# Reciprocal deviation of a layer norm: Ln and Exp on ScalarE in place of a power on GpSimd, with a new order of the work

## The chip, the cores and the metric

The kernel runs on one core of a Trainium2 chip. The core has five engines that work in parallel, each through its own queue in order: TensorE (matmuls, "PE" in the profile), VectorE ("DVE"), ScalarE ("ACT"), GpSimd ("POOL") and SyncE ("SP"), which issues the transfers. The metric is the time of one execution on the device in microseconds; lower is better.

## What is computed

Two transformer layers over 2048 rows of width 512. Each has a sliding-window attention (32 heads of 16, window 256) and a feed-forward part with relu; both read a layer norm of x and add to x.

```
def _layernorm(x, axis=-1, eps=1e-5):
    m = jnp.mean(x, axis=axis, keepdims=True)
    v = jnp.var(x, axis=axis, keepdims=True)
    return (x - m) / jnp.sqrt(v + eps)
...
    x = x + _A_ref(_layernorm(x, axis=-1), A_wqkv, A_wo)
    x = x + _B_ref(_layernorm(x, axis=-1), B_w1, B_w2)
    x = x + _A_ref(_layernorm(x, axis=-1), A_wqkv, A_wo)
    x = x + _B_ref(_layernorm(x, axis=-1), B_w1, B_w2)
```

In `_A_ref` the scores of q and k are scaled by 1/4, masked to the window, put through a softmax, multiplied with v and with `wo`. `_B_ref` is `relu(x @ w1) @ w2` with 1792 columns between.

## The kernel before

Rows go in chunks of 512, four chunks a layer, so there are eight steps k (k = 0 to 3 are the first layer). For each step the program plans: the norm of the chunk and the projections to q, k and v (`plan_qkv`, lines 542 to 609); the attention in units of one group of heads, 36 units with up to five score groups each (`plan_attention`, from 611); the output projection, the second norm and the feed-forward part (`plan_rest`, from 682). All of x stays in on-chip memory (`x_sb`), as do the weights.

A score group is four by two or three matmuls into the one score buffer `Sps`, followed by one exponential on ScalarE into `Pb` (line 633). The next scores need the buffer, so scores and exponentials alternate. The masks of the window work on `Pb` after the exponential, on VectorE or GpSimd (lines 440 to 458). The matmuls of attention with v (`acc`) need a whole unit's exponentials and masks. Between two score groups TensorE does other matmuls, if any is ready: projections (`ps_d<-xnT,wqk` and `wv`), output projection (`wo`) and feed-forward (`ps_d<-xn2T,w` and `w,hT`).

The norm of a block of 128 rows is a chain over several engines. `norm_stats` (line 332) makes mean and variance on VectorE (`bn_stats`, `bn_aggr` into `mvs`) and, for every second block, adds eps to two variances into `rstds`. `norm_pow` (356) raises these to the power -0.5 on GpSimd, two blocks at once, against a constant tile `mhalf`. `norm_apply` (360) writes the normalised block `xn`: on VectorE one operation with mean and reciprocal deviation; on GpSimd two small operations first, which make the negative mean times the reciprocal deviation (`nbs`), then one that multiplies and adds. A transposing DMA (SyncE's queue) or, for the first and the last chunk, TensorE's transposes bring `xn` into `xnT` or `xn2T`, which the matmuls read.

The order on each engine is not written out by hand. Every operation is an `Op` with a key, the engines that may do it with a time for each, and what it waits for. A small simulation (lines 777 to 898) runs through time with these durations (`EVAC`, the times beside the operations), a time for a signal from one engine to another (`LINK`), one for a freed buffer to be usable again (0.2 us) and times for TensorE to turn from one kind of matmul to another (`SWITCH`). Whenever an engine is free it takes, of the operations that are ready, the one with the smallest key plus ready time (`choose`, line 806), and that is how instructions are written into its queue. Some 100 numbers in `TUNE` shift the keys: `calm` those of the statistics of a chunk in the first layer, `apply` those of the applies, `mask`, `div`, `qkv`, `v`, `h`, `add` those of their operations; `lead` lets attention's matmuls start so long ahead of an exponential's end, `hold` keeps other matmuls back just ahead of it, and `slack` says how far another operation on ScalarE may reach into the time of the next exponential (`act_free`, line 824). If TensorE finds nothing for some time, a filler matmul ("warm") is put in. On the chip the queues run in that order, and semaphores decide the real times. All instructions go through a helper, so that nearly every row of the profile names its line, 152.

Of the kernel before, what the change touches and what calls it, by code (L numbers as in the profile page):

```python
# [14 lines left out]
ALU = mybir.AluOpType  # L15
P = 128
# [37 lines left out]
    ("qkv", 6): -0.16, ("qkv", 7): -14.32,
    ("v", 0): 13.35, ("v", 1): 3.92, ("v", 2): 26.56, ("v", 3): 18.45, ("v", 4): -13.88, ("v", 5): 7.52,
    ("v", 6): 18.09, ("v", 7): 3.4,
    ("h", 0): -6.3, ("h", 1): 14.4, ("h", 2): -21.08, ("h", 3): 6.8, ("h", 4): 11.71, ("h", 5): -2.12,
    ("h", 6): 9.91, ("h", 7): -16.5,
    ("mask", 0): -22.35, ("mask", 1): 12.42, ("mask", 2): 0.91, ("mask", 3): 7.99, ("mask", 4): 9.44,
    ("mask", 5): -27.11, ("mask", 6): -3.69, ("mask", 7): 8.01,  # L60
    ("div", 0): -20.69, ("div", 1): -29.64, ("div", 2): -11.92, ("div", 3): -2.95, ("div", 4): 7.05,
# [7 lines left out]
    ("pace", 6): -1.08, ("pace", 7): 4.91,
    ("from", 1): 13.51, ("from", 2): 36.31, ("from", 3): 0.92, ("from", 4): 5.3, ("from", 5): 11.42,  # L70
    ("from", 6): -38.65, ("from", 7): 33.44, ("from", (0, 0)): 2.38, ("from", (0, 2)): -18.94,
    ("span", 1): 67.18, ("span", 2): 34.97, ("span", 3): 28.32, ("span", 4): 54.36, ("span", 5): 52.47,
    ("span", 6): 24.91, ("span", 7): 70.78, ("span", (0, 0)): 35.26, ("span", (0, 2)): 58.29,
# [35 lines left out]
def kernel(  # L109
# [133 lines left out]
    LINK = {"PE": 0.2, "DVE": 0.2, "ACT": 0.2, "POOL": 0.2, "SP": 0.2}  # L243
# [50 lines left out]
    d_x = [landed(3.95), landed(4.5)]  # L294
    d_w = {1: landed(7.4), 0: landed(9.0), 2: landed(10.6)}
# [64 lines left out]
    def norm_apply(lid, j, src, deps, by_array, dst, then_key, dst_deps):  # L360
# [20 lines left out]
        return op(0, {"SP": (1.22, dma, 2.9)}, [a], None, [box])  # L381

    def transpose(key, src, dst, deps, uses, take=None):
# [671 lines left out]
```

## Time and profile before

| | |
|---|---|
| median of 3 runs | 465.89 us (464.25 to 467.16) |
| profiled execution, its own time | 466.79 us |
| its span, first to last instruction | 465.1 us |
| TensorE busy, matmuls | 439.3 us, 94% |
| VectorE busy | 362.6 us, 78% |
| ScalarE busy | 342.7 us, 74% |
| GpSimd busy | 324.4 us, 70% |
| mean granted clock of TensorE | 0.979 |

One execution is taken by the profiler. A busy share is a mean over the whole span; the stretches differ, so a table of stretches is read beside it. The granted clock is the share of TensorE's full speed in a stretch. In a row of instructions, out<-in are tiles by their names in the program, then partitions x elements and the type; the bracket at the end of a row tells for how long the engine idled before it and which instruction ended the wait. "issue" is time in which an engine waited for nothing that the profile shows.

### The profile page before, as it was taken

How to read it: one execution, taken by the hardware profiler on the slowest of the kernel's cores; microseconds unless marked ns; L12 is line 12 of the kernel's file. 1: busy time of each engine (PE TensorE's matmuls, PEld its weight loads, DVE VectorE, ACT ScalarE, POOL GpSimd, SP SyncE). 2: the span in 40 equal slices, each digit the busy share in tenths (PEclk: the TensorE clock that was granted, in tenths of full speed). 3: DMA queues.
4: the chain of work that ended last, by engine and by line, in shares of the span. 5: the costliest groups of instructions: out<-in, count | busy, mean ns of one | idle time of the engine just before them, and what ended most of it. 6: DMA issues, size and time to landing. Idle time of an engine off the chain costs nothing.

```text
span 465.1 us, 15122 instructions
## 1 busy us (share of the span) xinstructions
PE 439.3 (94%) x6418; PEld 216.4 (47%) x6418; DVE 362.6 (78%) x760; ACT 342.7 (74%) x278; POOL 324.4 (70%) x671
## 2 busy tenths in 40 slices
PE   7949988989699999999999999999999999999995
PEld 3625454644245454444544444454444445444443
DVE  6898888887878789988889888867987898669201
ACT  3877988678778887788877787888879887760530
POOL 3665788876878798889888778855886787741000
PEclk9997999899889999999999999999999999999999
DMA  8806101010302100211011102000041001100001
GB/s 259 274 13 184 25 1 26 13 37 2 47 14 59 24 3 14 35 24 25 1 39 35 24 3 47 4 2 1 24 82 35 4 13 48 35 1 24 23 15 39
DMA packets 39580, 18.36 MB, mean 39 GB/s; under 512 B 30928, under 2 KB 38992, under 8 KB 39504
## 3 DMA queue, kind: packets, MB, share of 16 engines
q1 hardware_dynamic: 39504, 17.31, 14.8%
q8 instruction: 52, 0.85, 0.8%
q14 instruction: 24, 0.20, 0.2%
HBM read 7.86 MB, written 2.10 MB: 21 GB/s over the span
## 4 chain that ended last, share of the span: by engine, by line
PE 81%; POOL 7%; ACT 4%; DMA 3%; issue 2%; DVE 1%; SPq 0%; POOLq 0%; ACTq 0%
PE ps_d L152 63%; PE Sps L152 10%; PE acc L152 8%; ACT Pb L152 4%; POOL Pb L152 4%; DMA Pb<-in_A_wqkv_dram 2%; POOL xn L152 1%; DMA xnT<-xn 1%; DMA xn2T<-xn 1%; POOL nbs L152 1%; POOL rstds L152 0%; SPq L152 0%; DVE st L152 0%; PE tp L152 0%; ACT wv L152 0%
## 5 line engine op out<-in xcount | busy, mean ns | idle before, releaser
L152 ACT ACTIVATE Pb<-Sps 128x2048 bf16<-128x2048 f32 (+2 forms) x156 | 282.7, 1812 | 68.4 <-PE Sps L152 48.4
L152 POOL TENSOR_SCALAR_AFFINE_SELECT Pb<-Pb 64x256 bf16<-64x256 bf16 x516 | 237.0, 459 | 72.8 <-ACT Pb L152 45.5
L152 PE MATMUL ps_d<-xn2T,w 128*128 128x512 bf16 (+1 forms) x504 | 109.7, 360 | 1.1 <-DMA xn2T<-xn 1.1
L152 PE MATMUL ps_d<-w,hT 128*128 128x512 bf16 (+1 forms) x462 | 106.8, 374 | 0.0
L152 PE MATMUL Sps<-Qt,KBD 32*128 32x320 bf16 (+3 forms) x1488 | 62.1, 254 | 13.5 <-ACT Pb L152 13.3
L152 PEld LDWEIGHTS <-w 128*128 128x128 bf16 x504 | 45.6, 99 | 48.9 <-issue 10.1
L152 PE MATMUL ps_d<-xnT,wqk 128*128 128x512 bf16 (+1 forms) x288 | 66.2, 361 | 2.3 <-DVE st L152 1.8
L152 PEld LDWEIGHTS <-hT 128*128 128x128 bf16 x462 | 41.6, 98 | 48.6 <-issue 6.6
L152 DVE TENSOR_TENSOR Pb<-Pb,tri 128x512 bf16<-128x512 bf16 (+1 forms) x132 | 56.2, 441 | 6.2 <-ACT Pb L152 5.5
L152 PEld LDWEIGHTS <-KBD 32*128 32x128 bf16 x1488 | 27.1, 93 | 69.9 <-issue 67.6
L152 DVE STREAM_TRANSPOSE TR<-acc 128x512 f32<-128x512 f32 (+1 forms) x72 | 44.6, 639 | 18.1 <-PE acc L152 17.7
L152 DVE TENSOR_SCALAR hT<-ps_d 128x512 bf16<-128x512 f32 (+1 forms) x73 | 43.9, 607 | 12.8 <-PE ps_d L152 12.0
L152 PE MATMUL acc<-Pb,V2f 64*32 64x320 bf16 (+4 forms) x2976 | 46.5, 256 | 0.6 <-POOL Pb L152 0.6
L152 DVE BATCH_NORM_STATS2 st<-x_sb 128x6 f32<-128x512 f32 (+1 forms) x64 | 43.8, 684 | 1.4 <-DMA x_sb<-in_A_x_dram 0.5
L152 PEld LDWEIGHTS <-V2f 64*32 64x32 bf16 x2976 | 35.8, 93 | 15.4 <-issue 8.4
L152 PEld LDWEIGHTS <-wqk 128*128 128x128 bf16 x288 | 24.8, 98 | 29.3 <-issue 9.9
L152 ACT ACTIVATE hT<-ps_d 128x512 bf16<-128x512 f32 (+1 forms) x53 | 29.6, 569 | 11.5 <-PE ps_d L152 10.9
L152 POOL TENSOR_TENSOR rstds<-rstds,mhalf 128x2 f32<-128x2 f32 (+1 forms) x33 | 25.0, 757 | 18.5 <-DVE rstds L152 16.4
L152 DVE TENSOR_TENSOR x_sb<-ps_d,x_sb 128x512 f32<-128x512 f32 x48 | 32.3, 679 | 6.2 <-PE ps_d L152 6.1
L152 PE MATMUL ps_d<-wv,xnT 128*64 128x256 bf16 x512 | 33.9, 276 | 0.5 <-ACT xnT L152 0.5
L152 PE MATMUL ps_d<-wo,OT 128*128 128x512 bf16 x128 | 33.0, 392 | 0.0
L152 DVE TENSOR_TENSOR ob<-ps_d,x_sb 128x512 bf16<-128x512 f32 (+1 forms) x17 | 11.2, 657 | 27.5 <-PE ps_d L152 27.5
(58 smaller groups left out, 313.2 us busy)
## 6 DMA issues: line engine op xcount, KB each, us to landing
out_dram<-ob SPq DMA_DIRECT2D x15, 128.0 KB, 1.7
w<-in_B_w_dram SPq DMA_DIRECT2D x1, 1792.0 KB, 12.7
w<-in_B_w_dram SPq DMA_DIRECT2D x2, 896.0 KB, 6.9
x_sb<-in_A_x_dram SPq DMA_DIRECT2D x3, 512.0 KB, 8.7
wqk<-in_A_wqkv_dram SPq DMA_DIRECT2D x2, 512.0 KB, 6.6
x_sb<-in_A_x_dram SPq DMA_DIRECT2D x2, 256.0 KB, 3.0
Pb<-in_A_wqkv_dram SPq DMA_DIRECT2D x1, 512.0 KB
wo<-in_A_wo_dram SPq DMA_DIRECT2D x1, 512.0 KB, 8.9
```

The source lines that it names most:

```text
L152: inst = fn(*a, **k)
```

## The change

Four things change together. First, the reciprocal deviation: ScalarE makes Ln of the variance with eps as its bias (a constant tile `epsb`), then Exp of -0.5 times that; the addition of eps on VectorE and the power on GpSimd go. Second, one VectorE operation per two blocks makes the negative mean times the reciprocal deviation into `nbs`, for every norm; GpSimd's two small operations ahead of its apply go. Third, the planner's times: many operations get two, until the engine is free and until the result is there; signals get a time for each pair of engines, and a freed buffer comes back after 0.06 us. Fourth, all the numbers of `TUNE`. The exact path at the end, which runs only where the softmax without maximum left the range, keeps the power.

The diff, cut to its core:

```diff
@@ -40,37 +40,37 @@
 PW = 512
 
 TUNE = {
-    ("lean", 0): -1.15, ("lean", 1): -1.98,
-    ("lead", 0): 1.36,
...
-    ("apply", 0): -19.87, ("apply", 1): 14.75, ("apply", 2): 0.1, ("apply", 3): -10.64, ("apply", 4): -33.85,
-    ("apply", 5): 7.29, ("apply", 6): -18.45, ("apply", 7): 51.67,
...
-    ("calm", 0): 107.76, ("calm", 1): 51.82, ("calm", 2): 482.67, ("calm", 3): 130.21,
...
+    ("lean", 0): 24.74, ("lean", 1): 4.71,
+    ("lead", 0): -0.27,
+    ("hold", 0): 0.22,
...
+    ("apply", 0): 89.38, ("apply", 1): 115.33, ("apply", 2): -9.09, ("apply", 3): 104.45, ("apply", 4): 60.26,
+    ("apply", 5): 53.44, ("apply", 6): 114.41, ("apply", 7): -65.26,
...
+    ("calm", 0): 721.99, ("calm", 1): 405.19, ("calm", 2): 965.51, ("calm", 3): 590.06,
...
@@ -195,6 +195,8 @@
     make_identity(nc, ident[:])
     mhalf = const.tile([P, 4], FP32, name="mhalf")
     dve.memset(mhalf[:], -0.5)
+    epsb = const.tile([P, 1], FP32, name="epsb")
+    dve.memset(epsb[:], 1e-5)
...
-    LINK = {"PE": 0.2, "DVE": 0.2, "ACT": 0.2, "POOL": 0.2, "SP": 0.2}
+    LINK = {"PE": {"PE": 0.0, "ACT": 0.2, "DVE": 0.2, "POOL": 0.2, "SP": 0.2},
+            "ACT": {"PE": 0.05, "ACT": 0.0, "DVE": 0.035, "POOL": 0.07, "SP": 0.1},
+            "DVE": {"PE": 0.06, "ACT": 0.06, "DVE": 0.035, "POOL": 0.1, "SP": 0.1},
+            "POOL": {"PE": 0.06, "ACT": 0.06, "DVE": 0.04, "POOL": 0.05, "SP": 0.1},
+            "SP": {"PE": 0.1, "ACT": 0.1, "DVE": 0.1, "POOL": 0.1, "SP": 0.0}}
+    FREED = 0.06
...
-            link = (0.05 if eng == "PE" else 0.08) if self.key < -9e4 else LINK[eng]
-            return max([t if e == eng else t + link for t, e in self.ends], default=0.0)
+            if self.key < -9e4:
+                return max([t if e == eng else t + (0.05 if eng == "PE" else 0.08) for t, e in self.ends], default=0.0)
+            return max([t + LINK[e][eng] for t, e in self.ends], default=0.0)
...
-    d_x = [landed(3.95), landed(4.5)]
-    d_w = {1: landed(7.4), 0: landed(9.0), 2: landed(10.6)}
+    d_x = [landed(3.65), landed(4.35)]
+    d_w = {1: landed(7.35), 0: landed(8.85), 2: landed(10.35)}
...
-    EVAC = {512: {"DVE": 0.71, "ACT": 0.6}, 256: {"DVE": 0.44, "ACT": 0.39}}
+    EVAC = {512: {"DVE": (0.61, 0.69), "ACT": (0.495, 0.6)}, 256: {"DVE": (0.37, 0.42), "ACT": (0.275, 0.385)}}
 
     def options(times, fn):
-        return {e: (t, lambda e=e: fn(e)) for e, t in times.items()}
+        return {e: (t[0], lambda e=e: fn(e), t[1]) for e, t in times.items()}
...
-            if eps_from is not None:
-                dve.tensor_scalar_add(rstds[:, lid % 8, eps_from:j + 1], mvs[:, lid % 8, eps_from:j + 1, 1], 1e-5)
-        return op(key, {"DVE": (0.91 + (0.22 if eps_from is not None else 0), fn)}, deps)
+        return op(key, {"DVE": (0.83, fn, 0.91)}, deps)
...
-        r = rstds[:, lid % 8, j0:j1]
-        return op(key, {"POOL": (0.75, lambda: pool.tensor_tensor(out=r, in0=r, in1=mhalf[:, j0:j1], op=ALU.pow))}, deps)
+        r, mv = rstds[:, lid % 8, j0:j1], mvs[:, lid % 8, j0:j1, :]
+
+        def fn():
+            act.activation(r, mv[:, :, 1], ACT.Ln, bias=epsb[:])
+            act.activation(r, r, ACT.Exp, scale=-0.5)
+        a = op(key, {"ACT": (0.34, fn, 0.45)}, deps)
+        return op(key, {"DVE": (0.1, lambda: dve.scalar_tensor_tensor(
+            out=nbs[:, lid % 8, j0:j1], in0=mv[:, :, 0], scalar=-1.0, in1=r, op0=ALU.mult, op1=ALU.mult), 0.14)}, [a])
...
-                pool.tensor_tensor(out=nb, in0=mv[:, 0:1], in1=r, op=ALU.mult)
-                pool.tensor_scalar(out=nb, in0=nb, scalar1=-1.0, scalar2=None, op0=ALU.mult)
                 pool.tensor_scalar(out=box.t[:], in0=src, scalar1=r, scalar2=nb, op0=ALU.mult, op1=ALU.add)
-        times = {"DVE": 0.52} if by_array else {"POOL": 1.6, "DVE": 0.63}
+        times = {"DVE": (0.43, 0.51)} if by_array else {"POOL": (1.56, 1.6), "DVE": (0.5, 0.58)}
...
-                exps[s] = op(-1e5, {"ACT": (0.176 + 0.00083 * 4 * (z - a), lambda u=u, g=g, pb=pb, cell=cell: exp_group(u, g, pb, cell["S"]))},
+                exps[s] = op(-1e5, {"ACT": (0.072 + 0.00083 * 4 * (z - a), lambda u=u, g=g, pb=pb, cell=cell: exp_group(u, g, pb, cell["S"]), 0.176 + 0.00083 * 4 * (z - a))},
...
-                    times = {"DVE": 0.36 + 0.15 * (len(m) - 1), "POOL": 0.95 * len(m)}
+                    times = {"DVE": (0.3, 0.375) if len(m) == 1 else (0.4, 0.48), "POOL": (1.0, 0.96) if len(m) == 1 else (2.05, 2.0)}
...
-    SWITCH = {"ds": 0.1, "sd": 0.1, "dv": 0.1, "vd": 0.25, "sv": 0.06, "vs": 0.02}
+    SWITCH = {"ds": 0.096, "sd": 0.085, "dv": 0.093, "vd": 0.22, "sv": 0.083, "vs": 0.25}
...
-                    b.pool.free.append((t + 0.2, b.index))
-                    push(t + 0.2, None, None)
+                    b.pool.free.append((t + FREED, b.index))
+                    push(t + FREED, None, None)
```

The other changed lines are of the same kinds: further numbers of `TUNE` and further times beside operations.

## Rows read from the trace of the kernel before

**Rows 1.** Page: busy us; costliest groups (us, mean ns | idle before, releaser).

```profile
PE 439.3 (94%) x6418; PEld 216.4 (47%) x6418; DVE 362.6 (78%) x760; ACT 342.7 (74%) x278; POOL 324.4 (70%) x671
...
L152 ACT ACTIVATE Pb<-Sps 128x2048 bf16<-128x2048 f32 (+2 forms) x156 | 282.7, 1812 | 68.4 <-PE Sps L152 48.4
...
L152 POOL TENSOR_TENSOR rstds<-rstds,mhalf 128x2 f32<-128x2 f32 (+1 forms) x33 | 25.0, 757 | 18.5 <-DVE rstds L152 16.4
```

**Rows 2.** Table of stretches: PE, PEld, DVE, ACT, POOL busy; PEclk, DMA, GB/s.

```profile
0.00:20.00 20.00, 17.15 (x186) 9.98 (x188) 14.54 (x47) 10.74 (x17) 9.92 (x25) 1.00 0.95 304
20.00:140.00 120.00, 104.06 (x1790) 56.02 (x1787) 99.21 (x230) 95.35 (x82) 91.79 (x190) 0.93 0.16 37
140.00:440.00 300.00, 298.81 (x4346) 140.49 (x4345) 245.88 (x480) 231.14 (x172) 222.67 (x458) 1.00 0.11 24
```

**Rows 3.** Table of stretches: weak places between 20 and 140 us.

```profile
24.00:36.00 12.00, 6.12 (x166) 3.27 (x165) 11.14 (x30) 8.78 (x9) 8.70 (x21) 0.87 0.01 3
32.00:40.00 8.00, 5.74 (x104) 2.36 (x103) 5.88 (x15) 4.50 (x4) 5.67 (x12) 0.57 0.25 46
76.00:84.00 8.00, 6.09 (x55) 3.06 (x53) 5.53 (x13) 4.43 (x3) 7.17 (x16) 0.80 0.17 36
...
120.00:128.00 8.00, 3.61 (x37) 1.26 (x37) 5.86 (x15) 5.63 (x3) 7.13 (x16) 0.82 0.45 68
128.00:132.00 4.00, 4.00 (x102) 1.75 (x100) 2.07 (x6) 1.84 (x2) 3.53 (x8) 0.51 0.00 0
```

**Rows 4.** TensorE's waits, 20 to 140 us: total us, times, longest.

```profile
PE Sps L152 <- ACT Pb L152: 13.0, 14, 1.4
```

**Rows 5.** Instructions in time, 28 to 38 us: start, us, engine, operation.

```profile
29.69 0.65 DVE L152 BATCH_NORM_STATS2 st<-x_sb 128x6 f32<-128x512 bf16 x1
...
30.59 0.17 DVE L152 TENSOR_SCALAR rstds<-mvs 128x2 f32<-128x2 f32 x1
...
32.77 0.72 POOL L152 TENSOR_TENSOR rstds<-rstds,mhalf 128x2 f32<-128x2 f32 x1
...
33.59 1.02 ACT L152 ACTIVATE Pb<-Sps 128x1024 bf16<-128x1024 f32 x1 [0.50 <-PE Sps L152]
...
35.75 0.76 POOL L152 TENSOR_SCALAR xn<-x_sb,rstds,nbs 128x512 bf16<-128x512 bf16 x1
```

**Rows 6.** Instructions in time, 69 to 84 us.

```profile
70.14 0.17 DVE L152 TENSOR_SCALAR rstds<-mvs 128x2 f32<-128x2 f32 x1
...
72.79 0.71 POOL L152 TENSOR_TENSOR rstds<-rstds,mhalf 128x2 f32<-128x2 f32 x1
...
80.63 3.06 PE L152 MATMUL ps_d<-xn2T,w 128*128 128x256 bf16 x14 [1.11 <-DMA xn2T<-xn]
```

**Rows 7.** Instructions in time, 112 to 134 us.

```profile
123.83 0.59 DVE L152 TENSOR_SCALAR xn<-x_sb,mvs,rstds 128x512 bf16<-128x512 bf16 x1 [1.70 <-POOL Pb L152]
```

**Rows 8.** Groups by shape: count, busy us, mean ns.

```profile
L152 ACT ACTIVATE hT<-ps_d 128x512 bf16<-128x512 f32 x46 | 27.1, 597 | 11.5 <-PE ps_d L152 10.9
...
L152 POOL TENSOR_SCALAR nbs<-nbs 128x1 f32<-128x1 f32 x32 | 9.0, 280 | 3.0
...
L152 DVE TENSOR_SCALAR rstds<-mvs 128x2 f32<-128x2 f32 x31 | 7.8, 253 | 1.1
...
L152 POOL TENSOR_TENSOR nbs<-mvs,rstds 128x1 f32<-128x1 f32 x32 | 6.9, 215 | 1.9
...
L152 ACT ACTIVATE hT<-ps_d 128x256 bf16<-128x256 f32 x7 | 2.5, 381 | 0.0
...
L167 ACT ACT_TABLE_LOAD x1 | 1.3, 1283 | 0.8 <-PEq L1039 0.8
...
L152 DVE SCALAR_TENSOR_TENSOR badacc<-chk_mn,chk_b 128x1 f32<-128x1 f32 x1 | 0.2, 159 | 0.0
```

**Rows 9.** GpSimd's waits for the eps sum: whole span, then 140 to 440 us.

```profile
POOL rstds L152 <- DVE rstds L152: 16.4, 8, 10.0
...
POOL rstds L152 <- DVE rstds L152: 12.9, 4, 10.0
```

More of the change, by code (lines that the diff above doesn't have):

```diff
@@ L54 @@
[L54 to L61, printed above, removed]
@@ L69 @@
[L69 to L73, printed above, removed]
+    ("lean", 0): 24.74, ("lean", 1): 4.71,
+    ("lead", 0): -0.27,
@@ new lines @@
+    ("hold", 0): 0.22,
+    ("ones", 0): 20.32,
+    ("tri", 0): 46.49,
+    ("turn", 0): 14.47,
+    ("apply", 0): 89.38, ("apply", 1): 115.33, ("apply", 2): -9.09, ("apply", 3): 104.45, ("apply", 4): 60.26,
+    ("apply", 5): 53.44, ("apply", 6): 114.41, ("apply", 7): -65.26,
+    ("idle", 0): 1.52,
+    ("slack", 0): 0.79, ("slack", 1): 0.35,
+    ("qkv", 0): 74.59, ("qkv", 1): -40.07, ("qkv", 2): -81.37, ("qkv", 3): 115.58, ("qkv", 4): -6.78,
+    ("qkv", 5): -132.95, ("qkv", 6): 40.01, ("qkv", 7): 110.02,
@@ new lines @@
+    ("v", 0): 26.3, ("v", 1): 17.55, ("v", 2): -110.02, ("v", 3): -79.77, ("v", 4): 16.37, ("v", 5): 1.09,
+    ("v", 6): 37.88, ("v", 7): 28.55,
+    ("h", 0): -14.89, ("h", 1): -47.23, ("h", 2): -144.09, ("h", 3): -49.97, ("h", 4): -14.77, ("h", 5): -57.87,
+    ("h", 6): 0.63, ("h", 7): 116.63,
+    ("mask", 0): -32.21, ("mask", 1): -12.77, ("mask", 2): 6.66, ("mask", 3): 46.18, ("mask", 4): -58.83,
+    ("mask", 5): -65.22, ("mask", 6): -11.34, ("mask", 7): -71.92,
+    ("div", 0): -77.16, ("div", 1): -3.34, ("div", 2): 125.58, ("div", 3): 123.55, ("div", 4): 69.83,
@@ new lines @@
+    ("div", 5): -35.41, ("div", 6): 137.9, ("div", 7): 77.04,
+    ("add", 0): 62.11, ("add", 1): 35.65, ("add", 2): -79.66, ("add", 3): -60.27, ("add", 4): -56.02,
+    ("add", 5): 30.35, ("add", 6): 81.67, ("add", 7): 84.36,
+    ("calm", 0): 721.99, ("calm", 1): 405.19, ("calm", 2): 965.51, ("calm", 3): 590.06,
+    ("wait", 1): -197.57, ("wait", 2): 45.45, ("wait", 3): 302.54, ("wait", 4): -22.15, ("wait", 5): -20.71,
+    ("wait", 6): -45.79, ("wait", 7): -85.42,
+    ("pace", 1): 0.2, ("pace", 2): 15.65, ("pace", 3): 113.65, ("pace", 4): -14.62, ("pace", 5): -83.67,
@@ L74 @@
+    ("pace", 6): -59.23, ("pace", 7): 13.97,
+    ("from", 1): 26.88, ("from", 2): 29.33, ("from", 3): 74.59, ("from", 4): 33.83, ("from", 5): 266.02,
+    ("from", 6): -0.61, ("from", 7): 31.66, ("from", (0, 0)): -18, ("from", (0, 2)): -15.68,
+    ("span", 1): 77.36, ("span", 2): 92.04, ("span", 3): 88.06, ("span", 4): 142.62, ("span", 5): 190.15,
+    ("span", 6): 67.72, ("span", 7): 13.87, ("span", (0, 0)): 140.83, ("span", (0, 2)): 70.77,
 }
@@ L389, in fn @@
                 pe.transpose(box.ps[:, kc, :], src()[:, kc * P:(kc + 1) * P], ident[:])
-        t = op(key, {"PE": (0.26, fn)}, deps, box, list(uses) + [box])
-        return op(0 if key != -5000 else tune("turn", 0, 0), options({"DVE": 0.42, "ACT": 0.59}, lambda e: copy(e, dst(), box.ps[:])), [t], take, [box])
+        t = op(key, {"PE": (0.24, fn)}, deps, box, list(uses) + [box])
+        return op(0 if key != -5000 else tune("turn", 0, 0), options({"DVE": (0.4, 0.48), "ACT": (0.49, 0.59)}, lambda e: copy(e, dst(), box.ps[:])), [t], take, [box])
     def slot(layer, kb):
@@ L527, in wv_part @@
         copy(e, wv[:, kc], wv_raw[:, kc].rearrange("p (a e d) -> p e a d", e=2, d=16))
-    c_wv = [op(tune("wv", 0, -2), options({"POOL": 0.8, "DVE": 0.6, "ACT": 0.6}, lambda e, kc=kc: wv_part(e, kc)), [d_w[2]]) for kc in range(KC)]
+    c_wv = [op(tune("wv", 0, -2), options({"POOL": (0.8, 0.75), "DVE": (0.55, 0.6), "ACT": (0.53, 0.63)}, lambda e, kc=kc: wv_part(e, kc)), [d_w[2]]) for kc in range(KC)]
     c_v = [op(tune("ones", 0, -2), {"DVE": (0.8, v_ones)})]
@@ L585, in plan_qkv @@
                 ev = op(soon("qkv", k), options(EVAC[w], kev), [m], ks, [box])
-                times = {"DVE": 0.75, "POOL": 3.4} if h is None else {"DVE": 0.54, "POOL": 2.1}
+                split = slot(layer, 8 * c) + h0 < NSLOT < slot(layer, 8 * c) + h1
+                times = {"DVE": (0.95, 1.0) if split else (0.67, 0.75), "POOL": (3.3, 3.35)} if h is None else \
+                    {"DVE": (0.37, 0.44), "POOL": (1.9, 1.95)}
                 k_done[k, t, h or 0] = op(soon("qkv", k), options(times, lambda e, t=t, h0=h0, h1=h1, ks=ks:
@@ L650, in pfn @@
                     pv_group(u, g, pb, accs, g == 0, g == len(u.groups) - 1)
-                us = sum(b[2] for b in u.groups[g]) * 0.0268
+                us = sum(b[2] for b in u.groups[g]) * 0.0268 + 0.005
                 end = g == len(u.groups) - 1
-                prior = op(-5e4 + n - (1000 if g else 0), {"PE": (us, pfn)},
+                prior = op(-5e4 + n - (1000 if g else 0), {"PE": (us, pfn, us + 0.13 if end else us)},
                            [prior] if g else need, accs if g == 0 else None, accs)
@@ L675, in bkfn @@
                 dve.transpose(out=ot[:, q0:q0 + w], in_=ob.t[:, 0:w])
[L676 removed]
+            m1 = op(soon("div", u.k), {"DVE": (0.11 + 0.00104 * w, bkfn, 0.16 + 0.00106 * w)}, [r1] + (wo_mm.get(k - 1, []) if u.t > 1 else wo_mm.get(k - 2, [])), None, [ob])
             for j in range(u.q0 // 2, u.q0 // 2 + u.nq // 2):
                 divs[k, u.t, j] = m1
[L679 removed]
+        checks.append(op(40, {"DVE": (0.55, lambda k=k: accumulate_check(chks[k % 2], k == 0))},
                          recips[k] + checks[-1:]))
@@ L699, in plan_rest @@
             wo_mm.setdefault(k, []).append(m)
-            add = op(soon("add", k), {"DVE": (0.69, lambda j=j, box=box: residual(4 * c + j, box.ps[:], layer == 0))}, [m], None, [box])
+            add = op(soon("add", k), {"DVE": (0.63, lambda j=j, box=box: residual(4 * c + j, box.ps[:], layer == 0), 0.69)}, [m], None, [box])
             single = final and j >= 2
```

31 lines of the change are left out of this document (8 added, 23 removed).

## The prediction

> **What bounds the kernel now.** I read the page's busy times first [rows 1]: TensorE is busy 439.3 us, 94% of the span, against 362.6 for VectorE. So TensorE is the bound on average, and the question is where its other 25.8 us are. The table of stretches answers it [rows 2]: from 140 to 440 us TensorE is busy 298.81 of 300 us, so nothing that another engine does faster there can move the end. From 20 to 140 us it is busy 104.06 of 120: 15.94 us idle. In the first 20 us it idles 2.85; the rest lies at the way out.
>
> Next, the same table for the weak places inside 20 to 140 [rows 3]. Idle TensorE is 5.88 us in 24 to 36, 1.91 in 76 to 84, 4.39 in 120 to 128; together 12.18 of the 15.94. Each is joined by a stretch with a lower granted clock: 0.57 over 32 to 40, 0.80 over 76 to 84, 0.51 over 128 to 132. Of TensorE's two levels (2.4 and 1.2 GHz) that is partly or wholly the lower one, after idling. What it took: (1 - 0.57) x 5.74 busy us = 2.5, (1 - 0.80) x 6.09 = 1.2, (1 - 0.51) x 4.00 = 2.0, and (1 - 0.82) x 3.61 = 0.6 in 120 to 128; 6.3 us in all. So 15.9 + 6.3 = 22.2 us is about the most that a better order can win in this stretch.
>
> Who lets TensorE run dry? Its waits in that stretch are nearly all for the exponential, 13.0 us in 14 waits [rows 4]. It waits for the exponential because no projection or feed-forward matmul is ready to go between two score groups; those need a normalised chunk. The instructions in order of time show how such a chunk arrives. At 24 to 36: VectorE makes the last statistics of chunk 1 from 29.69 and their sum with eps until 30.59 + 0.17; the power starts on GpSimd at 32.77, 2.0 us later and with no idle time ahead of it: the engine was still at the masks queued in front; two small nbs operations go ahead of each apply, and the second apply starts at 35.75 [rows 5]. At 76 to 84: the sum with eps ends at 70.14 + 0.17, the power starts at 72.79, 2.5 us later, again without idle time, and TensorE's feed-forward matmuls start at 80.63, released by the transposing DMA that follows the applies [rows 6]. At 120 to 128 an apply on VectorE stands 1.70 us for GpSimd, which is in its masks [rows 7]. GpSimd is not the bound, but its in-order queue carries the norm chain behind masks, and the norm chain feeds the bound where spare matmuls are short.
>
> **The change, part by part.** Each is costed by instructions first, then by the wait it shortens.
>
> *GpSimd loses* the power, 33 instructions, 25.0 us [rows 1], and both small nbs steps, 32 each, 6.9 + 9.0 us [rows 8]: 40.9 us. By itself this is worth nothing in 140 to 440, since TensorE is full there.
>
> *VectorE loses* 33 additions of eps, 253 ns in the common form, and gains 33 scalar_tensor_tensor for the negative mean times the reciprocal deviation. The one such operation in the trace, on one column, takes 159 ns [rows 8]; by these two rows 33 x 0.16 = 5.3 to 33 x 0.25 = 8.3 us come for 8.3 that go: a gain of 3 at best, even at worst. I take 0, for VectorE's last step sets no end that I could read.
>
> *ScalarE gains* 33 pairs, Ln then Exp, on two columns. Its relu copies take 597 ns on 512 columns and 381 ns on 256 [rows 8]: 0.84 ns a column and some 165 ns to start with. Below: 2 x 0.165 = 0.33 us a pair. Above: two of 256 columns, 0.76 us. I take 0.35, near the lower end, because two columns are nearest to the intercept. 33 x 0.35 = 11.6 us on a ScalarE that idles 68.4 us ahead of its exponentials [rows 1]; that idle time hides it as long as the pair sits between two exponentials. In 20 to 140, with a share of 120/465 of the norms, that is 8.5 pairs; if their cover is gone they cost 8.5 x 0.35 = 3.0 us (at 0.76, 6.5 us).
>
> The Trainium skill, "ScalarE: Activation LUTs", section "What ACT_TABLE_LOAD costs", speaks a little against this part: it gives 186 ns plus 0.833 ns an element, 93 ns more for a bias read from a pointer (as Ln has it here) and 93 ns of overlap, so a pair would be about 0.37 us by an estimate from that page. The copies of the trace bear out the slope (0.84). By it the 11.6 us would be 12.3; nothing below rests on it.
>
> *The norm chain.* New: the sum with eps and the power become the pair on ScalarE (0.35), then one VectorE step (0.16), then the apply. A pair can also have to sit out one exponential, 1.81 us in the mean [rows 1]. At the first stall the old way from the sum with eps (30.76) to the second apply (35.75) is 4.99 us. New 0.51 to 2.32 and the first apply's 0.76: saved 1.9 to 3.7. At the second: from 70.31 to the power's end at 72.79 + 0.71, and 0.50 for the nbs steps, 3.69 us; saved 1.4 to 3.2. At the third I count only the nbs steps of two applies, 2 x 0.50 = 1.0 us. Sum 4.3 to 7.9; I take the middle, 6.1 us of idle TensorE. The low clock goes with the idling: 6.3 us for 12.18 idle, 0.52 for each, so 3.2 us more. This holds only if the order lets the step shorten; if what is late next is VectorE's statistics, it is nothing (a rival below).
>
> *The start.* The first two powers on GpSimd (757 ns in the mean) give way to pairs. TensorE idles 2.85 us in the first 20, part of it before anything can be there, so a gain between 0 and 1 us; I take 0.5.
>
> *The order.* The planner gets operation times nearer to the trace: VectorE and ScalarE are counted free some 0.1 us before a result is there, signals cost 0.035 to 0.2 us by pair of engines and not 0.2 throughout, a freed buffer returns after 0.06 and not 0.2 us, and 100 or so keys are new. The trace can't price an order. Bounds: it wins the whole of what is left, 22.2 - 6.1 - 3.2 = 12.9; or it makes one more stall as dear as the dearest seen, 24 to 40 us: 5.88 + 2.5 = 8.4 us of loss. I take the middle of the two, a gain of 2.2. For more: truer times let the planner see the room that VectorE and ScalarE have. For less: keys of ±100 us move the statistics of later chunks to the very back (calm 52 to 405 for chunk 1, 483 to 966 for chunk 2), and those are what came late. That attention's matmuls now go after an exponential's end and not 1.36 us ahead of it (lead) touches 36 units; no row prices it, and it is left inside these bounds.
>
> **Sum.** The profiled execution took 466.79 us for a span of 465.1. 466.8 - 6.1 - 3.2 - 0.5 - 2.2 = 454.8. The median of the runs is 465.89, 0.9 below the profiled one: 453.9, so 454 us, 2.6% less. A difference of about 1% is what a measurement of this kernel can tell from none.
>
> **Rivals.**
> *A: the order fills the stretch.* All 22.2 us go: 465.9 - 22.2 = 443.7, about 444; with the start's whole 1 us, 442.7. For it: the norms of the later chunks in the first layer need only x, which is loaded early, so there is work to fill with. Against: VectorE is busy 11.14 of 12 us at 24 to 36 [rows 3], and has to make those statistics.
> *B: the gap stays.* VectorE's statistics are late, not the power: at the first stall the last of chunk 1 start only at 29.69 [rows 5], and masks still stand in front of applies on GpSimd. Then only the nbs steps at the third stall (1.0 us) and the start (0.5) are won: 464.4. For it speaks VectorE's 93% there; against it, that the power stood 2.0 and 2.5 us behind masks with its operand ready.
> *C: the wait moves into ScalarE's queue.* Ln must wait for the statistics, and the engine is in order: a pair issued before its statistics are done holds the next exponential, then the scores. Before, GpSimd stood 16.4 us for the eps sum, 12.9 of them in 140 to 440 where TensorE is full [rows 9]; 3.5 us remain. With these and the pairs' own 3.0 us uncovered in 20 to 140 and nothing won: 465.9 + 3.5 + 3.0 = 472.4. It decides from 4.7 us on. For it: at the first stall the exponential of 33.59 starts 0.50 us after the last has ended [rows 5], so a pair of 0.35 us with its signals fills that cover. Against: over the whole span 48.4 us of the 68.4 are waits for scores [rows 1], so most pairs are covered.
> *D: table switches.* One table load is in the trace, 1283 ns [rows 8], and Ln has not run behind it. If Ln and Exp each reloaded, 66 x 1.283 = 84.7 us on ScalarE, in front of the exponentials: about 550. By the Trainium skill, "ScalarE: Activation LUTs", section "Table sets: the hidden batching unit", ln and exp lie together in one set, the one that this kernel names at its start, so there would be none; no run here shows Ln yet.
>
> **How the numbers follow.** The forecast's own kind (chain shorter, order between its bounds) 0.50, with its own range 446 to 461; A 0.14; B 0.19; C 0.15; D 0.02. Faster by over 1% (under 461.2): 0.50 + 0.14 = 0.64. Within 1%: 0.19. Slower (over 470.6): 0.15 + 0.02 = 0.17. The range goes from 442, A's end, to 472, C's price: beyond it lie some 0.05 of A, 0.08 of C and D's 0.02.
>
> **What would show it.** Right: TensorE's idle time in 20 to 140 us falls from 15.9 to near 9 us, and the stretches at a lower clock get fewer; GpSimd's busy time falls by about 41 us, unless it is given more masks; a pair takes about 0.35 us; 140 to 440 stays full. Wrong: idle unchanged and the statistics of the next chunk just as late (B); exponentials that start late behind a Ln (C); more than one table load (D). If TensorE's busy time itself falls by more than the clock accounts for, the order changed the switches between score, attention and other matmuls, which I priced at nothing.

## The result and the profile after

The changed kernel takes 451.2 us (450.79 to 453.52), where the kernel before took 466.5 in the same runs: a ratio of 0.969, 95% interval 0.964 to 0.974. The span of its profiled execution is 449.6 us, against 465.1.

The page of the changed kernel: busy time of each engine, then two of the costliest groups.

```profile
PE 432.8 (96%) x6423; PEld 215.4 (48%) x6423; DVE 362.8 (81%) x787; ACT 351.6 (78%) x340; POOL 269.9 (60%) x501
...
L152 ACT ACTIVATE Pb<-Sps 128x2048 bf16<-128x2048 f32 (+2 forms) x156 | 282.4, 1810 | 46.9 <-PE Sps L152 36.0
L152 POOL TENSOR_SCALAR_AFFINE_SELECT Pb<-Pb 64x256 bf16<-64x256 bf16 x428 | 197.4, 461 | 108.5 <-ACT Pb L152 86.1
```

VectorE's sum is the same. ScalarE has 8.9 us more, GpSimd 54.5 us less: more than the 41 us of the removed steps, because the new order also gives it fewer masks (428 for 516) and fewer applies (23 for 32), which outweigh more spreads of k (36 for 12). The table of stretches, columns as in [rows 2]:

```profile
0.00:20.00 20.00, 17.41 (x165) 10.53 (x165) 14.99 (x49) 11.96 (x22) 7.15 (x21) 1.00 0.89 300
20.00:140.00 120.00, 112.36 (x2010) 61.38 (x2009) 109.34 (x257) 105.77 (x110) 89.43 (x145) 1.00 0.24 45
140.00:440.00 300.00, 299.38 (x4223) 140.62 (x4221) 236.91 (x480) 233.83 (x210) 173.29 (x337) 1.00 0.10 22
```

Against [rows 2], TensorE's idle time from 20 to 140 us goes from 15.94 to 7.64 us, 8.30 less; the granted clock there goes from 0.93 to 1.00, so the 6.3 us of the low clock are gone whole; the first 20 us give 0.26, the stretch to 440 us 0.57. 8.30 + 6.3 + 0.26 + 0.57 = 15.4 of the 15.5 us between the spans. (The 6.3 us are worked out from the granted clocks before; TensorE's busy time falls by 439.3 - 432.8 = 6.5 us, which fits.) So nearly all that was won was won where [rows 3] had its weak places, before 140 us, and the rest of the program moved forward by it: the last exponential begins at 396.48 us, not at 410.07. All three weak places take part: idle TensorE goes from 7.35 to 3.21 us in 20 to 60 us, from 2.70 to 0.00 in 60 to 100 and from 5.89 to 4.43 in 100 to 140. TensorE's waits for the exponential in 20 to 140 us, 13.0 us in [rows 4]:

```profile
PE Sps L152 <- ACT Pb L152: 3.9, 5, 1.3
```

The new operations, groups by shape (count, busy us, mean ns, idle before):

```profile
L152 ACT ACTIVATE rstds<-mvs,epsb 128x2 f32<-128x2 f32 x31 | 9.1, 293 | 13.1 <-DVE mvs L152 13.0
...
L152 DVE SCALAR_TENSOR_TENSOR nbs<-mvs,rstds 128x2 f32<-128x2 f32 x31 | 6.6, 213 | 1.1 <-ACT rstds L152 1.1
L152 ACT ACTIVATE rstds<-rstds 128x2 f32<-128x2 f32 x31 | 6.3, 203 | 1.0
```

A pair is 0.293 + 0.203 = 0.50 us. ScalarE stands 13.0 us in all for VectorE's statistics with a pair at the head of its queue; 4.5 us of these lie in the first 20 us and 7.6 behind the last exponential, 0.9 between 140 and 400 us.

### The profile page after: what moved, and what is told of

It reads as the page before. It is cut to its first block, busy times and chain, and to the rows that moved or that the text cites. A ratio compares the mean times of both kernels' runs of the same rounds, so it can differ in the third digit from the quotient of the medians.

```text
span 449.6 us, 15005 instructions
## 1 busy us (share of the span) xinstructions
PE 432.8 (96%) x6423; PEld 215.4 (48%) x6423; DVE 362.8 (81%) x787; ACT 351.6 (78%) x340; POOL 269.9 (60%) x501
## 4 chain that ended last, share of the span: by engine, by line
PE 83%; DVE 6%; ACT 5%; DMA 3%; issue 1%; SPq 0%; ACTq 0%; DVEq 0%
PE ps_d L152 64%; PE Sps L152 10%; PE acc L152 8%; ACT Pb L152 5%; DMA Pb<-in_A_wqkv_dram 2%; DVE Pb L152 1%; DVE x_sb L152 1%; DMA xnT<-xn 1%; DVE st L152 1%; DVE xn L152 1%; DVE Qt L152 1%; SPq L152 0%; DVE TR L152 0%; ACT rstds L152 0%; DVE Kst L152 0%
## 5 line engine op out<-in xcount | busy, mean ns | idle before, releaser
L152 POOL TENSOR_SCALAR_AFFINE_SELECT Pb<-Pb 64x256 bf16<-64x256 bf16 x428 | 197.4, 461 | 108.5 <-ACT Pb L152 86.1
L152 DVE TENSOR_TENSOR Pb<-Pb,tri 128x512 bf16<-128x512 bf16 (+1 forms) x157 | 66.5, 433 | 9.8 <-ACT Pb L152 9.4
L152 PE MATMUL Sps<-Qt,KBD 32*128 32x320 bf16 (+3 forms) x1488 | 60.9, 251 | 6.0 <-ACT Pb L152 4.1
L152 PEld LDWEIGHTS <-KBD 32*128 32x128 bf16 x1488 | 26.0, 92 | 66.4 <-issue 63.5
L152 POOL TENSOR_SCALAR KBD<-Kst,par 128x512 bf16<-128x512 bf16 (+1 forms) x36 | 50.0, 1401 | 4.7 <-DVE Kst L152 3.2
L152 DVE TENSOR_SCALAR hT<-ps_d 128x512 bf16<-128x512 f32 (+1 forms) x68 | 40.8, 614 | 5.7 <-PE ps_d L152 5.6
L152 PE MATMUL acc<-Pb,V2f 64*32 64x320 bf16 (+4 forms) x2976 | 44.2, 251 | 0.0
L152 ACT ACTIVATE hT<-ps_d 128x512 bf16<-128x512 f32 (+1 forms) x58 | 31.6, 553 | 11.4 <-PE ps_d L152 11.1
L152 PE MATMUL ps_d<-wv,xnT 128*64 128x256 bf16 x512 | 35.1, 276 | 0.4 <-ACT V2f L152 0.4
L152 PE MATMUL ps_d<-wo,OT 128*128 128x512 bf16 x128 | 30.7, 380 | 0.0
```

The source lines that it names most:

```text
L152: inst = fn(*a, **k)
```

## The experiments

Twelve kernels, each timed against the kernel before on the same chip. All ratios are to it.

| kernel | operations | times | keys | planned | median us | ratio (95% interval) |
|---|---|---|---|---|---|---|
| changed kernel | new | new | new | | 451.2 | 0.969 (0.964 to 0.974) |
| `ops_old_order` | new | old | old | held | 466.6 | 1.000 (0.998 to 1.003) |
| `old_ops_new_order` | old | new | new | held | 455.5 | 0.978 (0.974 to 0.981) |
| `keys_only` | old | old | new | anew | 470.6 | 1.011 (1.009 to 1.014) |
| `times_only` | old | new | old | anew | 466.4 | 1.002 (1.000 to 1.005) |
| `all_but_keys` | new | new | old | anew | 468.2 | 1.006 (1.004 to 1.008) |
| `ops_and_keys` | new | old | new | anew | 474.3 | 1.021 (1.015 to 1.027) |
| `times_and_keys` | old | new | new | anew | 458.4 | 0.987 (0.983 to 0.992) |
| `early_stats` | old | old | one key new | anew | 467.7 | 1.007 (1.005 to 1.009) |
| `late_stats` | new | new | new, one wait more | anew | 456.0 | 0.983 (0.977 to 0.988) |
| `pair_twice` | new, pair doubled | new | new | held | 458.0 | 0.987 (0.983 to 0.991) |
| `pair_left_out` | new, no pair | new | new | held | 451.9 | 0.973 (0.968 to 0.977) |
| `power_on_gpsimd` | old power, new nbs step | new | new | held | 470.9 | 1.013 (1.009 to 1.017) |

"Held" means that the planner ran as in the kernel named and only the instructions that it writes at a place were exchanged, so every queue keeps its order; an instruction that goes to another engine enters that engine's queue at the same place of the program, which the planner did not plan for it. "Anew" means that the planner made another order. In the traces of most of these runs one matmul record in a hundred is missing, so TensorE's busy time in them reads low; the start of an instruction and the granted clock are used instead.

### The operations in the old order

```diff
-            if eps_from is not None:
-                dve.tensor_scalar_add(rstds[:, lid % 8, eps_from:j + 1], mvs[:, lid % 8, eps_from:j + 1, 1], 1e-5)
...
-        r = rstds[:, lid % 8, j0:j1]
-        return op(key, {"POOL": (0.75, lambda: pool.tensor_tensor(out=r, in0=r, in1=mhalf[:, j0:j1], op=ALU.pow))}, deps)
+        r, mv = rstds[:, lid % 8, j0:j1], mvs[:, lid % 8, j0:j1, :]
+
+        def fn():
+            act.activation(r, mv[:, :, 1], ACT.Ln, bias=epsb[:])
+            act.activation(r, r, ACT.Exp, scale=-0.5)
+            dve.scalar_tensor_tensor(out=nbs[:, lid % 8, j0:j1], in0=mv[:, :, 0], scalar=-1.0, in1=r, op0=ALU.mult, op1=ALU.mult)
+        return op(key, {"POOL": (0.75, fn)}, deps)
...
-                pool.tensor_tensor(out=nb, in0=mv[:, 0:1], in1=r, op=ALU.mult)
-                pool.tensor_scalar(out=nb, in0=nb, scalar1=-1.0, scalar2=None, op0=ALU.mult)
```

> The new norm operations in the old order: wherever the old order had a power on GpSimd, Ln, Exp and the one VectorE step are written at that place of the program; eps addition and the two nbs steps are gone; planner, its times and its keys are those of before. Theory of the forecast (the operations shorten the norm chain): 9 us off, about 457 us, and the first projection matmul of chunk 1 starts at about 38 us, not 41.4. Rival (the gain is the order: chunk 1's statistics are made some 10 us earlier): 464 to 466 us, TensorE idle in 20 to 140 us within 1.5 us of 15.9. Rival C (the wait moves into ScalarE's queue): 468 or more.

Measured: 466.6 us, ratio 1.000 (0.998 to 1.003), next to the first rival (464 to 466). The operations by themselves win nothing in the old order. The instructions in order of time at the first stall show why, first ScalarE's, then TensorE's first matmul on chunk 1:

```profile
32.45 1.88 ACT L152 ACTIVATE Pb<-Sps 128x2048 bf16<-128x2048 f32 x1 [0.76 <-PE Sps L152]
34.22 0.29 ACT L152 ACTIVATE rstds<-mvs,epsb 128x2 f32<-128x2 f32 x1
34.54 0.20 ACT L152 ACTIVATE rstds<-rstds 128x2 f32<-128x2 f32 x1
34.83 1.02 ACT L152 ACTIVATE Pb<-Sps 128x1024 bf16<-128x1024 f32 x1
```

```profile
42.47 1.28 PE L152 MATMUL ps_d<-wv,xnT 128*64 128x256 bf16 x20
```

[rows 5] had the power at 32.77, two microseconds behind masks. Here the last statistics start at 31.02, the pair lies behind the exponential of 32.45 and begins at 34.22. One queue was left and another joined: ScalarE's exponential takes as long as GpSimd's masks did. The next exponential then starts at 34.83. From the start of the last statistics to the end of the pair it is 34.54 + 0.20 - 31.02 = 3.7 us, where the power was done after 32.77 + 0.72 - 29.69 = 3.8. The first matmul on chunk 1's normalised rows is at 42.47, where it was at 41.63. The granted clock of 20 to 140 us stays at 0.93.

VectorE's queue is joined too. Its nbs step now stands where the pair does, and VectorE waits there for the pair 25 times, 30.5 us in all (12.4 us in 20 to 140); in the changed kernel, whose planner knows the step, it is 2 times and 1.1 us. The first long wait is early:

```profile
17.04 0.16 DVE L152 SCALAR_TENSOR_TENSOR nbs<-mvs,rstds 128x2 f32<-128x2 f32 x1 [1.95 <-ACT rstds L152]
```

The program is about 1 us late from there on, and so are the statistics of 31.02 (29.69 before). So the result of 1.000 holds for the operations in an order that was not made for them. Planned anew alone they were not run.

### The old operations in the new order

```diff
+            if eps_from is not None:
+                dve.tensor_scalar_add(rstds[:, lid % 8, eps_from:j + 1], mvs[:, lid % 8, eps_from:j + 1, 1], 1e-5)
...
         def fn():
-            act.activation(r, mv[:, :, 1], ACT.Ln, bias=epsb[:])
-            act.activation(r, r, ACT.Exp, scale=-0.5)
+            pool.tensor_tensor(out=r, in0=r, in1=mhalf[:, j0:j1], op=ALU.pow)
         a = op(key, {"ACT": (0.34, fn, 0.45)}, deps)
-        return op(key, {"DVE": (0.1, lambda: dve.scalar_tensor_tensor(
-            out=nbs[:, lid % 8, j0:j1], in0=mv[:, :, 0], scalar=-1.0, in1=r, op0=ALU.mult, op1=ALU.mult), 0.14)}, [a])
+        return op(key, {"DVE": (0.1, lambda: None, 0.14)}, [a])
...
+                pool.tensor_tensor(out=nb, in0=mv[:, 0:1], in1=r, op=ALU.mult)
+                pool.tensor_scalar(out=nb, in0=nb, scalar1=-1.0, scalar2=None, op0=ALU.mult)
```

> The order of the changed kernel with the old norm operations written at the same places: power on GpSimd where the pair was, eps addition behind the statistics, two nbs steps ahead of GpSimd's applies, nothing on ScalarE. Theory of the forecast: 451 + 9 = 460 us. Rival (the order carries it): 451 to 454 us, TensorE idle in 20 to 140 us below 10.

Measured: 455.5 us, 0.978 (0.974 to 0.981), between the two expectations and nearer to the order's. The order alone is worth 2.2%, some 10 us, without one new operation. The new operations are worth the rest, 451.2 against 455.5, but only in this order, which was made for them. Whether keys found anew for the old operations would do as well was not tried. The first matmul on chunk 1 is at 31.12:

```profile
31.12 0.61 PE L152 MATMUL ps_d<-xnT,wqk 128*128 128x512 bf16 x1
```

### Keys, times and operations apart

Each kernel puts one or two of the three parts (operations, times, keys) from the changed kernel into the kernel before and plans anew.

```
 keys_only:      - TUNE of before        + TUNE of after
 all_but_keys:   - TUNE of after         + TUNE of before
 times_only:     + LINK, FREED, EVAC, SWITCH and all times of after; operations and TUNE of before
 ops_and_keys:   + operations and TUNE of after; times of before (pair 0.45 us, nbs step 0.14 us)
 times_and_keys: + times and TUNE of after; operations of before (power 0.75 us on GpSimd)
```

> Before with the 100 new keys alone, old times and old operations, planned anew. If the keys carry the order: 453 us or below. If keys are only good together with the times they were found with: 466 to 485 us, because they then describe another order.

Measured: 470.6 us, 1.011 (1.009 to 1.014), as the second reading had it.

> The changed kernel with the old keys: new operations and new times, planned anew. If truer times alone make the order better: 455 us or below. If keys and times belong together: 466 us or more.

Measured: 468.2 us, 1.006 (1.004 to 1.008). New operations and truer times, with the old keys, are 0.6% slower than before.

> Before with the new operations and the new keys, but the old times (signals of 0.2 us throughout, one time for each operation, buffers back after 0.2 us), planned anew. If keys and operations carry the order: 453 us or below. If keys belong to the times with which they were found: 462 to 470 us.

Measured: 474.3 us, 1.021 (1.015 to 1.027): the worst of all, beyond both expectations.

> Before with the new times alone; old operations, old keys, planned anew. If truer times alone help: 460 us or below. If they do nothing without keys that fit: 464 to 470 us.

Measured: 466.4 us, 1.002 (1.000 to 1.005): nothing.

> The changed kernel's times and keys with the old norm operations, which the planner now knows of (power 0.75 us on GpSimd, eps with the statistics), so that it plans anew. If the new order's gain does not need the new operations: 452 to 457 us, as with the old operations in the held order (455.5). If keys only fit the plan for which they were found: 462 to 470 us.

Measured: 458.4 us, 0.987 (0.983 to 0.992); with the same parts in the held order it was 455.5. It lies between the two expectations, near the first.

So no part is good by itself. Only keys and times together gain, and then the operations add to it. The corner with the operations alone, planned anew, was not run. What the parts do to the first stall, read from the instructions in order of time of each trace (start, us):

| kernel | last statistics of chunk 1 | first projection matmul of chunk 1 | first feed-forward matmul of chunk 0 | granted clock, 20 to 140 us | median us |
|---|---|---|---|---|---|
| before | 29.69 | 41.63 | 56.65 | 0.93 | 466.5 |
| `ops_old_order` | 31.02 | 42.47 | 57.48 | 0.93 | 466.6 |
| `keys_only` | 30.48 | 41.70 | 57.43 | 0.94 | 470.6 |
| `ops_and_keys` | 31.42 | 42.02 | 61.32 | 0.96 | 474.3 |
| `times_only` | 18.89 | 26.74 | 56.93 | 0.94 | 466.4 |
| `all_but_keys` | 18.49 | 31.63 | 53.44 | 0.93 | 468.2 |
| `times_and_keys` | 19.40 | 29.09 | 54.52 | 0.97 | 458.4 |
| `old_ops_new_order` | 18.94 | 31.12 | 49.74 | 0.99 | 455.5 |
| changed kernel | 19.29 | 31.50 | 49.16 | 1.00 | 451.2 |

The truer times bring the statistics forward by 11 us with either set of keys, and the old times do not with either set; which of the times does it was not tried. But that alone is worth nothing (`times_only`). What the keys add is the next piece: with them the feed-forward part of chunk 0 is 4.3 us earlier with the new operations (49.16 for 53.44) and 2.4 us with the old ones planned anew (54.52 for 56.93). The three fastest kernels of the table are the three with the highest clock here and, but for `all_but_keys`, with the earliest feed-forward part.

The table follows the first stall only, and idle time alone does not tell all: a filler counts as busy. In 20 to 140 us `ops_and_keys` has 30 fillers, 8.5 us busy, 22 of them in 100 to 140; the kernel before has 7, 2.0 us.

### When chunk 1's statistics are made

The first stall of [rows 3] has VectorE's last statistics of chunk 1 at 29.69 [rows 5]. In the changed kernel they are at 19.29, and the projections begin at 31.50. Instructions in order of time of the changed kernel, VectorE, then the chunk's second pair on ScalarE, then TensorE:

```profile
19.29 0.68 DVE L152 BATCH_NORM_STATS2 st<-x_sb 128x6 f32<-128x512 bf16 x1
...
26.79 0.58 DVE L152 TENSOR_SCALAR xn<-x_sb,mvs,rstds 128x512 bf16<-128x512 bf16 x1
```

```profile
20.33 0.29 ACT L152 ACTIVATE rstds<-mvs,epsb 128x2 f32<-128x2 f32 x1
20.66 0.20 ACT L152 ACTIVATE rstds<-rstds 128x2 f32<-128x2 f32 x1
```

```profile
31.50 1.67 PE L152 MATMUL ps_d<-xnT,wqk 128*128 128x512 bf16 x7 [0.53 <-DMA xnT<-xn]
```

```profile
48.07 1.25 PE L152 MATMUL ps_d<-xnT,wqk 128*128 128x512 bf16 x5
49.16 1.04 PE L152 MATMUL ps_d<-xn2T,w 128*128 128x256 bf16 x8
```

From the start of these statistics to the chunk's last apply it is 26.79 - 19.29 = 7.5 us. In the kernel before the same way was 35.75 - 29.69 = 6.1 [rows 5]. The pair itself comes sooner: it is done 20.66 + 0.20 - 19.29 = 1.6 us after the start of the statistics, where the power took 3.8. But the last apply has its place in VectorE's queue only at 26.79, so the whole way did not get shorter. It started 10 us earlier. Two kernels move the start alone:

```diff
 early_stats (before):
-    ("calm", 1): 51.82
+    ("calm", 1): -150
 late_stats (changed kernel):
+            if k == 1 and j == 3:
+                came = came + [exps[8]]
```

> Before with one key changed: calm of chunk 1 from 51.82 to -150, so that the planner gives chunk 1's statistics to VectorE at once (the last of them right behind the third, not some 15 us later); all else is planned anew from there. If the late statistics of chunk 1 are the cause of the first stall and the order is otherwise as good: its 5.9 us of idle and 2.5 us of low clock go, 457 to 459 us. If the gain needs the whole set of keys: 463 to 470 us.

Measured: 467.7 us, 1.007 (1.005 to 1.009). The last statistics of chunk 1 start at 14.73, TensorE has its matmuls on chunk 1 at 29.04, twelve microseconds before the old order, and nothing is won. Instructions in order of time on TensorE, then a row of the table of stretches:

```profile
29.04 1.61 PE L152 MATMUL ps_d<-wv,xnT 128*64 128x256 bf16 x26
...
45.46 1.90 PE L152 MATMUL ps_d<-xnT,wqk 128*128 128x512 bf16 x8
47.65 0.29 PE L152 MATMUL Sps<-Qt,KBD 32*128 32x256 bf16 x4 [0.29 <-ACT Pb L152]
...
51.96 1.03 PE L152 MATMUL warm<-ident 128*128 128x512 bf16 x2
...
56.51 1.25 PE L152 MATMUL ps_d<-xn2T,w 128*128 128x256 bf16 x5
```

```profile
52.00:60.00 8.00, 6.03 (x98) 2.48 (x96) 6.13 (x18) 4.85 (x4) 6.75 (x16) 0.50 0.16 36
```

The projections of chunk 1 are used up at 47.4. The feed-forward part of chunk 0 is ready only at 56.51, so TensorE runs dry from 47.6 on and does fillers, and the low clock comes with it (0.50 over 52 to 60 us). The stall was not filled, it moved by some 20 us. In the changed kernel the same feed-forward matmuls begin at 49.16, and projections of chunk 1 last up to there: the five before them start at 48.07.

> The changed kernel, where the planner may start the last statistics of chunk 1 only after the ninth exponential (about where the old order had them, some 13 us later than its own); all else is planned anew. If those statistics decide: 451 + 8 = 459 us, with the first projection of chunk 1 at about 41 us. If the order is good for other reasons: 451 to 454 us.

Measured: 456.0 us, 0.983 (0.977 to 0.988), 5 to 6 us worse than the changed kernel by the medians and by the ratios: between the two expectations. The last statistics of chunk 1 start at 32.19, its first projection at 40.12:

```profile
40.12 1.03 PE L152 MATMUL ps_d<-xnT,wqk 128*128 128x512 bf16 x4
```

So this one start is worth a third of the gain or somewhat more where everything behind it fits, and nothing where the next piece of work is late. Planning anew moves other work too: the feed-forward part of chunk 0 begins at 55.89 here. Both pieces are then about as late as in the kernel before, and still more than half of the gain is there. Most of that half lies behind the first stall: idle TensorE in 60 to 140 us is at most 4.77 us here, against 8.59 before, and in 20 to 60 at most 6.84, against 7.35.

### What a pair costs

```diff
 pair_twice:
+            act.activation(spare, mv[:, :, 1], ACT.Ln, bias=epsb[:])
+            act.activation(spare, spare, ACT.Exp, scale=-0.5)
             act.activation(r, mv[:, :, 1], ACT.Ln, bias=epsb[:])
             act.activation(r, r, ACT.Exp, scale=-0.5)
 pair_left_out:
-            act.activation(r, mv[:, :, 1], ACT.Ln, bias=epsb[:])
-            act.activation(r, r, ACT.Exp, scale=-0.5)
+            dve.tensor_scalar_add(r, mv[:, :, 1], 1e-5)
```

> The changed kernel in its own order, with each Ln and Exp pair run twice (first into a spare tile that nobody reads). 33 pairs of about 0.5 us more on ScalarE. If the pairs are covered by the wait for scores or by other matmuls on TensorE: 451 to 452 us. If they delay the loop of exponentials where TensorE has nothing else (the stretch of 20 to 140 us): about 11 x 0.5 = 5.5 us more, 456 to 457. If all are on the path: 467.

Measured: 458.0 us, 0.987 (0.983 to 0.991), 7 to 8 us more than the changed kernel. The price is near the second expectation, but most of it lies elsewhere: TensorE's waits for exponentials grow from 3.9 to 6.2 us in 20 to 140, and more in the stretch that was full. TensorE's waits from 140 to 400 us, first the changed kernel, then this one:

```profile
PE Sps L152 <- ACT Pb L152: 0.2, 1, 0.2
```

```profile
PE Sps L152 <- ACT Pb L152: 4.8, 11, 0.9
```

The stretch in which TensorE was full is not full any more: it stands 4.8 us for exponentials there. In the same order the changed kernel is busy 259.38 of these 260 us, so there are matmuls to do, but TensorE's queue is in order too, and the scores stand at its head.

> The changed kernel in its own order, without Ln and Exp: an addition of eps on VectorE stands at their place, so the reciprocal deviation is not computed and the rows are scaled otherwise; all other work is there. If the pairs' price is the same from one to two as from none to one (doubling them cost about 8 us, half of their 16 us): 443 us. If the order has room for one pair and none for two: 449 to 451 us.

Measured: 451.9 us, 0.973 (0.968 to 0.977), the same as with the pair within the intervals (VectorE does 33 additions more here). So the price is not a straight line: the order has room for one pair at each place and not for two.

### The power on GpSimd, with the new nbs step

```diff
-            act.activation(r, mv[:, :, 1], ACT.Ln, bias=epsb[:])
-            act.activation(r, r, ACT.Exp, scale=-0.5)
+            dve.tensor_scalar_add(r, mv[:, :, 1], 1e-5)
+            pool.tensor_tensor(out=r, in0=r, in1=mhalf[:, j0:j1], op=ALU.pow)
```

> The changed kernel in its own order, with the addition of eps on VectorE and the power on GpSimd in place of the pair; the VectorE step for nbs stays, so GpSimd's small steps stay away. All old operations in this order took 455.5 us, against 451.2 with the new. If the power's stand in GpSimd's queue makes these 4 us: 455. If the small nbs steps make them: 451 or a little below. If the pairs on ScalarE cost as the doubling says: 446 to 448.

Measured: 470.9 us, 1.013 (1.009 to 1.017), none of the three. It is 15 us worse than all the old operations in the same order. The waits of VectorE, longest in total:

```profile
DVE ob L152 <- PE ps_d L152: 25.3, 9, 14.4
DVE nbs L152 <- POOL rstds L152: 23.9, 24, 2.7
DVE TR L152 <- PE acc L152: 19.5, 16, 2.9
```

The nbs step needs the power, and VectorE stands for it 24 times, 23.9 us. In 9 of these waits, 15.3 us, GpSimd is still at masks or spreads of k. In the other 15, 8.7 us, the power began as soon as the eps sum was there, and VectorE stands for the power itself (0.72 us). GpSimd in turn stands 36.3 us for VectorE's eps sums, in 19 of 33. Two things differ from the old operations in the same order: the nbs step on VectorE, and the eps addition, which stood behind the statistics there and stands at the pair's place here (GpSimd's wait for it was 20.0 us there). So that VectorE's standing makes the 15 us is likely, and not shown; which of the two does it stays open. Nor is the nbs step free behind Ln and Exp as such: it stood 1.1 us in the changed kernel and 30.5 us in `ops_old_order`. A power on VectorE was not tried.

## Why the prediction was right, and where it was not

It said 454 us, 442 to 472, faster with 0.64. It was 451.2.

**The place** was right: nearly all is won before 140 us, as [rows 2] and [rows 3] had it, and about by the sum that was named: idle 15.9 to 7.6 us (forecast near 9), and a clock that stays at 1.00.

**The low clock** was put too small: 3.2 us by the rate of 0.52 for each us of idle, where all 6.3 went. 8.3 us of idle went and the whole of the low clock with them; the idle that is left (1.9 us of the 4 from 104 to 108 us are the emptiest) stands at a granted clock of 1.00. A rate read from the mean over three stalls did not hold for what stayed.

**The norm chain** (6.1 us, and the 3.2 of clock) is the step that failed. It took the new operations to shorten the way from statistics to apply, at the old place in time. `ops_old_order` is the nearest run to that step alone: 0. What the forecast set as 0.35 us and at most one exponential of waiting was that exponential at the first stall, as long as the masks that it left behind, and the forecast had nothing for the nbs step that waits for the pair in VectorE's queue, 30.5 us there. In the changed kernel the pair is done sooner, 1.6 us for 3.8, but the way to the last apply is longer, 7.5 us for 6.1, and the gain at this stall came from its start.

**The order** (2.2 us, set as the middle between two bounds) is the term that carried it: 455.5 us with the old operations, some 10 us. It lies inside the bound of 12.9 that was named. The reason for a low value, that the statistics of later chunks had been moved to the very back by `calm`, was wrong: they came at 19.29 us in spite of a `calm` of 405, and at 18.89 with the old key and the new times. Between these kernels their place follows the times; the key can move them too (14.73 in `early_stats`), but a larger one did not send them back. The 2.2 us, as the middle of two bounds, rested on no row that prices an order. So two terms of the sum changed places, 9.3 and 2.2 against 0 and 10, and 4 more where both are in; the sum hid it, and that the total came near is luck.

**The start** (0.5 us) gave 0.26 us of idle TensorE in the first 20 us.

**The pair** takes 0.50 us, not 0.35: ScalarE's intercept from the copies, 165 ns, was good for Exp (203 ns) only roughly and not for Ln with its bias (293 ns), and Exp has to wait for Ln. The Trainium skill, "ScalarE: Activation LUTs", section "What ACT_TABLE_LOAD costs", gives 93 ns for a bias read from a pointer; the 90 ns between Ln and Exp agree, though no run has one function with and without it. The same section of the Trainium skill gives 93 ns of overlap for activations back to back. That is not seen where the second needs the first: Exp starts at 20.66, 0.33 us after the start of a Ln of 0.29. Where it does not, it is: in `ops_old_order` the exponential of 32.45 ends at 34.33 and Ln starts at 34.22.

**The rivals.** A (all 22 us) did not come, but two thirds of it did. B (VectorE's statistics are late, not the power) named what was late at the first stall and went wrong on the outcome, since the order could cure it; but early statistics alone won nothing (`early_stats`). C (the wait moves into ScalarE's queue) did not come in the changed kernel, where a pair stands 0.9 us for statistics from 140 to 400 us and not at all in 20 to 140. At the first stall of `ops_old_order` it is the other way round: the pair of 34.22 waits behind an exponential and holds none up, since the scores for the next are done at 34.78. Only the pairs' own price is real, in `pair_twice` (7 us). The argument against C, that waits for scores cover the pairs, holds for one pair at each place only. D did not come: there is one table load of 1283 ns, as before, with Ln and Exp running behind it. The Trainium skill, "ScalarE: Activation LUTs", section "Table sets: the hidden batching unit", puts ln and exp into one set, and this one load agrees.

What stays open: which of the 100 keys bring the feed-forward part of chunk 0 forward, and how much of the gain it carries by itself. No kernel moved it alone. Nor was it followed what in the order cured the second and third stall, about half of the gain.

## What to carry to other kernels

Before an operation is moved to another engine to get it out of a queue, look at what stands in the new engine's queue at that very time: here an exponential took the place of the masks, and the exchange alone was worth nothing. Look also at what waits for it: a small step at the wrong place of VectorE's queue stood 30.5 us. When a bound engine runs dry, filling the first gap is not enough; the work after it has to be early too, or the gap moves. And keys that steer a planner hold only with the times that they were found with: change one and find the other anew, or expect a loss, here 0.6 to 2.1 per cent.

## What the runs showed of the hardware

VectorE's one small step (31 of them, 6.6 us busy in the changed kernel) stood 23.9 us in 24 waits behind a power on GpSimd, 30.5 us in 25 behind Ln and Exp in an order not planned for it, and 1.1 us in 2 where it was planned. Doubling 33 pairs of small operations on ScalarE (16 us busy) cost 7 to 8 us although TensorE had matmuls to do: its waits for exponentials grew from 3.9 to 6.2 us in 20 to 140 us and from 0.2 to 4.8 in 140 to 400. Ln and Exp on two columns took 293 and 203 ns, one behind the other. And 7.64 us of idle TensorE in 120 us cost no clock at all in the changed kernel, where 15.94 us before cost 6.3.
